# Last block of a fused retention and PReLU kernel: a second group of d_ff tiles by seven products, the second-layer products in another order, the third sums on GpSimd

## The chip, the core and the metric

The kernel runs on one core of one Trainium2 chip. The core has five engines with a queue each, taken in order: TensorE (PE in the profile, with its weight loads as PEld), VectorE (DVE), ScalarE (ACT), GpSimd (POOL) and SyncE (SP, which here only issues transfers). The metric is device time in microseconds (us) of one execution; the times given are medians of several.

## The reference

Eight heads of 64 run a decaying recurrence over 768 steps for four batches; the 3072 rows of 512 that come out go through a two-layer network with a leaky rectifier of its own slope for each of the 2048 hidden columns.

```python
for t in range(S):
    state = gamma * state + einsum('bhd,bhe->bhde', k[:, :, t], v[:, :, t])
    y[:, :, t] = scale * einsum('bhd,bhde->bhe', q[:, :, t], state)
x = y.transpose(0, 2, 1, 3).reshape(B * S, H * D)     # 3072 x 512
h = x @ w_in                                          # d_ff = 2048
g = maximum(h, 0) + alpha * minimum(h, 0)
out = g @ w_out                                       # 3072 x 512, float32
```

## The kernel before

The 3072 rows are worked through in `NBLK` = 6 blocks of 512 rows (n = 0 to 5). A block passes through a first layer (its 512 rows of x, kept transposed as `xT`, times `w_in`, giving `gt`, the hidden values after the rectifier, as 16 tiles f of 128 hidden columns) and a second layer (`gt` times `w_out`). The recurrence of block n+1 is computed in chunks inside the second layer of block n, so that in block 5 nothing but the two layers is left. The order of work on every engine is the order of the calls in the program; a generator is advanced with `tick(gen, m)` by m matmuls.

**First layer of blocks 3 to 5** (`ffn1_mix`). A "full" tile takes four matmuls of 128x512 (`L923`), a negated relu on ScalarE into `hm` (`L906`) and a multiply-add on VectorE (`L910`) that writes `gt`. One group of four tiles (0, 1, 8 and 9) is instead formed by seven products of half-size operands (a Strassen-Winograd scheme) of four 128x256 matmuls each (`L953`, numbers 1 to 7 in `part`). It reads sums of pieces of `w_in` (`wins`, from `win_sum`, formed once on GpSimd in block 2) and sums of pieces of x (`xsum`, from `x_sum`, formed for each block: two on VectorE, two on GpSimd). The products pile up in three PSUM banks; after numbers 1, 6 and 7 ScalarE copies a bank out (`kept`, `L966`), and the next product into that bank waits for that copy. After 2, 7 and 3 VectorE adds another bank to a copy (`L970`); the rectifier of such a sum is a relu on ScalarE some steps later and a pair of operations on GpSimd (`L983`, `L989`), in `ends`. `MIX` says which step is a product of the group and which (0) a full tile.

**Second layer of blocks 1 to 5** (`seven`). Again seven products, each of 16 matmuls of 128x256 (`L790`), first for 128 rows (t = 0) over the eight tiles f, then for the other 128. The operands are quarters of `gt` (`A(i, j)`: rows half i, tiles half j) and of `w_out`, and sums of these: `gs` 0 and 1 (`sm[0]`, `sm[1]`), `third`, and an in-place difference in `gt`, formed by `g_sums(n, part, which, engine)`, where `part` is a half of the tiles (f 0 to 3, or 4 to 7) and `which` is 0 to 3 in that order. In block 5, `gs` 0 and 1 of part 0 are begun inside the first layer (GpSimd, then VectorE), the rest is on VectorE. The order of the products in block 5 is: A(0,0); A(0,1); `sm[1]`; `sm[0]`; `third`; A(1,1); A(0,1) after its in-place difference. Results leave PSUM by ScalarE copies (`kept`, `L808`) and VectorE sums (`os`, `put`, `L820`), and then by stores (`L824`).

`minus` (`L738`) is the one line that records all sums of both kinds; they are told apart by the names of their tiles.

```python
MIX = [1, 2, 0, 5, 6, 0, 7, 0, 0, 4, 3] + 8 * [0]
fts = [f for i in range(2, HF) for f in (i, i + HF)]     # full tiles: 2, 10, 3, 11, ... 7, 15
```

Of the kernel before, what the change touches and what calls it, by code (L numbers as in the profile page):

```python
# [19 lines left out]
def kernel(  # L20
# [761 lines left out]

    def seven(n):
        gt, sm = gts[n], gsum[n]

        def product(bank, a, w, first=False):
            for t in range(2):
                for f in range(HF):
                    bk = bank[t] if isinstance(bank, list) else bank
                    nc.tensor.matmul(  # L790
                        out=bk[:, 256 * t : 256 * t + 256],
                        lhsT=a[:, f, 128 * t : 128 * t + 128],
                        rhs=w[:, f, :],
                        start=first and f == 0 and (t == 0 or bk is not bank),
                        stop=(f == HF - 1),
                        skip_group_check=True,
                    )
                    yield
# [12 lines left out]
        end = n + 1 == NBLK  # L811
# [40 lines left out]
        if end:  # L852
            gen = product(c, A(0, 1), W(1, 1))
            for _ in range(HF):
                yield next(gen)
            store()
            put(0, 1, c, u2, ts=(0,), store=nc.sync)()
            yield from gen
            put(0, 1, c, u2, ts=(1,))()
        else:  # L860
            yield from product(c, A(0, 1), W(1, 1))
            store()
            late_stores.append(put(0, 1, c, u2))

    wins, xsum = [], []

    def win_sum(i, eng):  # L870
        if not wins:
            wins.append(sbp.tile([128, 4, 2, 256], F16, tag="gs2", bufs=1, name="wins"))
        t = wins[0]
        a = [[w_in_all[:, 2 * l : 2 * l + 2, 1024 * j : 1024 * j + 256] for l in range(2)] for j in range(2)]
# [19 lines left out]
        minus(eng, t[:, i], x, y)  # L894


    MIX = [1, 2, 0, 5, 6, 0, 7, 0, 0, 4, 3] + 8 * [0]

    def ffn1_mix(n):
        fts = [f for i in range(2, HF) for f in (i, i + HF)]  # L900
        x = xT[n]
        h, bk, later = {}, {}, []

# [27 lines left out]
            prelu(ft, slice(0, TB), relu(hps, "hm"), hps)  # L931


        def part(s, i):
# [4 lines left out]
            b, w, t = bk[at], wins[0], xsum[0]  # L939
            for ff in range(2):  # L940
                f = slice(128 * ff, 128 * ff + 128)
                f8 = slice(1024 + 128 * ff, 1152 + 128 * ff)
                for kk in range(2):
                    lhsT, rhs = (
                        (w_in_all[:, kk, f], x[:, 0, kk, :]),
                        (w_in_all[:, 2 + kk, f], x[:, 0, 2 + kk, :]),
                        (w[:, 3, kk, f], x[:, 1, 2 + kk, :]),
                        (w_in_all[:, 2 + kk, f8], t[:, 3, kk, :]),
                        (w[:, 0, kk, f], t[:, 0, kk, :]),
                        (w[:, 1, kk, f], t[:, 1, kk, :]),  # L950
                        (w[:, 2, kk, f], t[:, 2, kk, :]),
                    )[i - 1]
                    nc.tensor.matmul(  # L953
                        out=b[:, 256 * ff : 256 * ff + 256],
                        lhsT=lhsT,
                        rhs=rhs,
                        start=first and ff == 0 and kk == 0,
                        stop=kk == 1,
                        skip_group_check=True,
                    )  # L960
                    yield
            if i in (1, 6, 7):
                h[i] = sbp.tile(
                    [128, 512], FP, tag="um1" if i == 6 else "um0", bufs=2, name="kept"
                )
                nc.scalar.activation(out=h[i], in_=b, func=COPY, bias=0.0, scale=1.0)  # L966
            if i in (2, 7, 3):

                to = h[{2: 1, 7: 7, 3: 6}[i]]
                nc.vector.tensor_tensor(out=to, in0=bk["a" if i == 2 else "c"], in1=to, op=ADD)  # L970
                later.append((s, to, {2: (0, 0), 7: (HF, 256), 3: (0, 256)}[i]))
            if i == 4:
                hm = relu(b, "hm")
                for ff in range(2):
                    at = slice(256 * ff, 256 * ff + 256)
                    prelu(HF + ff, slice(0, 256), hm[:, at], b[:, at])

        def ends():
            while later:
                _, to, (f, t) = later.pop(0)  # L980
                hm = relu(to, "uv")
                hv, v = [a.rearrange("p (f t) -> p f t", f=2) for a in (hm, to)]
                nc.gpsimd.tensor_tensor(  # L983
                    out=hv,
# [5 lines left out]
                    out=gt_at(n, slice(f, f + 2), slice(t, t + 256)), in0=hv, in1=v, op=ADD  # L990
                )

        for s, step in enumerate(MIX):
            yield from part(s, step) if step else full()
# [256 lines left out]
    for n in range(1, NBLK):  # L1251
        more = n + 1 < NBLK
        u0 = UB * (n + 1)
        if n == 2:
# [12 lines left out]
                tick(gen, (14, 14, 6, 16)[i])  # L1267
            g_sums(n, 0, 2, G)
            for i in range(4):
                win_sum(i, G)  # L1270
            for _ in gen:
                pass
        elif n > 2:
            gen = ffn1_mix(n)
            tick(gen, 8)
            flush(late_stores)
            if more:
# [20 lines left out]
        if not more:  # L1298
            tick(gen, 4 * HF + 2)
# [2 lines left out]
        if more:  # L1302
# [118 lines left out]
```

## Time and profile before

| | before |
|---|---|
| time, median of 3 runs | 199.31 us (198.13 to 200.34) |
| span of the profiled execution | 196.5 us |
| PE busy | 188.7 us (96%) |
| VectorE busy | 151.4 us (77%) |
| GpSimd busy | 149.0 us (76%) |
| ScalarE busy | 119.1 us (61%) |

The times are taken without the profiler and hold more than the span, which runs from the first to the last instruction of one execution; that execution has no other time of its own than its span. The median is 2.8 us above it. A busy PE is not a PE at its peak. In rows of the timeline the columns are: start, length, engine, line, operation, output and inputs with their shape, count, and in brackets the idle time before it with what ended it.

### The profile page before, as it was taken

What the parts mean: (1) busy time and instruction counts of PE and PEld (TensorE: products, weight loads), DVE (VectorE), ACT (ScalarE), POOL (GpSimd) and SP (SyncE); (2) the same over time, 40 slices, a digit from 0 to 9 for tenths busy, and PEclk for the clock granted to TensorE, in tenths of its full rate; (3) what the DMA queues carried; (4) which work ended last, traced back from release to release, by engine and by line L of the source; (5) the groups of instructions that cost most, each with busy time, mean ns of one, the idle gap of its engine ahead of it and who ended that gap; (6) DMA issues with size and microseconds to landing.
All of it is one profiled execution on the core that took longest, in us unless ns stands there. A gap on an engine that the chain in (4) does not pass through costs nothing.

```text
span 196.5 us, 6453 instructions
## 1 busy us (share of the span) xinstructions
PE 188.7 (96%) x2668; PEld 131.3 (67%) x2668; DVE 151.4 (77%) x258; ACT 119.1 (61%) x265; POOL 149.0 (76%) x151
## 2 busy tenths in 40 slices
PE   7879999999999989999999999999999999999993
PEld 5657544558668878644788754888654888655882
DVE  2697987164989897588978879967789977798922
ACT  3377763238676954477549987749987334686210
POOL 3368989999999576999379999499999296678000
PEclk9999999999999999999999999999999999999999
DMA  6999999999898999999998999992860013100014
GB/s 170 326 361 400 408 384 284 328 360 195 180 244 132 184 306 225 212 282 240 226 222 201 213 224 224 244 215 83 184 189 2 3 57 110 57 0 0 0 58 160
DMA packets 92749, 38.78 MB, mean 197 GB/s; under 512 B 70176, under 2 KB 88624, under 8 KB 92720
## 3 DMA queue, kind: packets, MB, share of 16 engines
q1 hardware_dynamic: 91440, 37.36, 75.8%
q10 hardware_dynamic: 1280, 1.01, 1.6%
q8 instruction: 21, 0.34, 0.7%
q14 instruction: 8, 0.07, 0.1%
HBM read 27.35 MB, written 6.29 MB: 171 GB/s over the span
## 4 chain that ended last, share of the span: by engine, by line
PE 75%; DVE 5%; POOL 5%; DMA 4%; ACT 3%; issue 2%; SPq 2%; POOLq 1%; DVEq 0%; ACTq 0%
PE ops L790 25%; PE hps L620 12%; PE hps L923 11%; PE hps L648 9%; PE ops L715 5%; PE hps L953 3%; DMA qu<-in_q_dram 2%; SPq L340 2%; POOL gt L989 2%; ACT kq L129 2%; PE ops L684 2%; DMA kt<-kq 2%; POOL hm L983 2%; PE ya L522 1%; POOLq L1416 1%
## 5 line engine op out<-in xcount | busy, mean ns | idle before, releaser
L790 PEld LDWEIGHTS <-gt 128*128 128x128 f16 x320 | 30.6, 98 | 4.1
L923 PE MATMUL hps<-xT,win 128*128 128x512 f16 x144 | 33.0, 379 | 0.0
L910 DVE SCALAR_TENSOR_TENSOR gt<-hm,small,hps 128x512 f16<-128x512 f32 (+1 forms) x42 | 28.7, 706 | 5.1 <-ACT hm L906 3.8
L790 PE MATMUL ops<-wout,gt 128*128 128x256 f16 x240 | 28.4, 273 | 0.0
L906 ACT ACTIVATE hm<-hps 128x512 f32<-128x512 f32 x39 | 23.1, 593 | 6.1 <-PE hps L923 5.4
L620 PE MATMUL hps<-xT,win 128*128 128x512 f16 x112 | 24.5, 379 | 0.0
L630 DVE SCALAR_TENSOR_TENSOR gt<-hm,small,hps 128x512 f16<-128x512 f32 x28 | 20.9, 747 | 3.8 <-ACT hm L629 0.9
L923 PEld LDWEIGHTS <-win 128*128 128x128 f16 x144 | 14.1, 98 | 14.4
L137 POOL TENSOR_TENSOR kq<-kqs,tab 128x512 f16<-128x512 f32 x23 | 23.6, 1050 | 0.0
L629 ACT ACTIVATE hm<-hps 128x512 f32<-128x512 f32 x28 | 16.7, 597 | 9.3 <-PE hps L620 9.3
L662 DVE SCALAR_TENSOR_TENSOR gt<-hm,small,hps 128x256 f16<-128x256 f32 x40 | 17.1, 477 | 4.3 <-ACT hm L657 4.3
L808 ACT ACTIVATE kept<-ops 128x512 f32<-128x512 f32 x15 | 9.0, 597 | 18.4 <-PE ops L790 18.4
L620 PEld LDWEIGHTS <-win 128*128 128x128 f16 x112 | 11.0, 98 | 12.8
L217 POOL TENSOR_TENSOR t<-ss,tab 128x256 f16<-128x256 f32 x13 | 8.7, 670 | 14.0 <-DVE ss L215 14.0
L790 PE MATMUL ops<-wsum,gs 128*128 128x256 f16 x160 | 19.1, 273 | 0.2 <-DVE os L820 0.2
L738 POOL TENSOR_TENSOR gt<-gt,gs 128x1024 f16<-128x1024 f16 x8 | 17.0, 2125 | 2.3 <-PE ops L790 2.3
L648 PE MATMUL hps<-xT,win 128*128 128x256 f16 x160 | 18.3, 273 | 0.0
L129 ACT ACTIVATE kq<-kqs,tab 128x64 f16<-128x64 f32 x72 | 18.1, 337 | 0.0
L648 PEld LDWEIGHTS <-win 128*128 128x128 f16 x160 | 15.4, 98 | 2.4
L790 PEld LDWEIGHTS <-gs 128*128 128x128 f16 x160 | 15.1, 98 | 2.4 <-issue 0.4
L820 DVE TENSOR_TENSOR os<-ops,kept 128x512 f32<-128x512 f32 (+1 forms) x17 | 10.5, 624 | 6.5 <-ACT kept L808 4.6
L657 ACT ACTIVATE hm<-hps 128x512 f32<-128x512 f32 x20 | 11.8, 597 | 5.5 <-PE hps L648 3.9
(132 smaller groups left out, 388.5 us busy)
## 6 DMA issues: line engine op xcount, KB each, us to landing
out_dram<-os SPq DMA_DIRECT2D x20, 256.0 KB, 3.5
wi<-in_moe_w_in_dram SPq DMA_DIRECT2D x8, 512.0 KB, 7.7
wo<-in_moe_w_out_dram SPq DMA_DIRECT2D x8, 512.0 KB, 8.5
kqs<-in_k_dram SPq DMA_DIRECT2D x16, 256.0 KB, 4.3
kqs<-in_q_dram SPq DMA_DIRECT2D x16, 256.0 KB, 4.2
vs<-in_v_dram SPq DMA_DIRECT2D x16, 256.0 KB, 4.9
ku<-in_k_dram SPq DMA_DIRECT2D x4, 256.0 KB, 4.1
qu<-in_q_dram SPq DMA_DIRECT2D x4, 256.0 KB, 4.7
```

The source lines that it names most:

```text
L129: eng.activation(out=kqs[u][:, a, h % 4, h // 4, :], in_=staged[u][nm][:, h, :], func=COPY, bias=0.0, scale=tab[:, H * a + h : H * a + h + 1],
L137: eng.tensor_tensor(out=kqs[u][:, a].rearrange("p i r d -> p r i d"), in0=staged[u][nm].rearrange("p (r i) d -> p r i d", i=4), in1=tab[:, ...
L620: nc.tensor.matmul(out=hps, lhsT=w_in_all[:, hp, 128 * ft : 128 * ft + 128], rhs=xT[n][:, :, hp, :], start=(hp == 0), stop=(hp == 3),)
L629: nc.scalar.activation(out=hm, in_=hps, func=RELU, bias=0.0, scale=-1.0)
L630: nc.vector.scalar_tensor_tensor(out=gt_at(n, ft, slice(0, TB)), in0=hm, scalar=oma_sb[:, ft : ft + 1], in1=hps, op0=MULT, op1=ADD,)
L648: nc.tensor.matmul(out=hps[:, 256 * (ft - f0) : 256 * (ft - f0) + 256], lhsT=w_in_all[:, hp, 128 * ft : 128 * ft + 128], rhs=xT[n][:, half ...
L662: nc.vector.scalar_tensor_tensor(out=gt_at(n, f, to), in0=hm[:, at], scalar=oma_sb[:, f : f + 1], in1=hps[:, at], op0=MULT, op1=ADD,)
L738: eng.tensor_tensor(out=out, in0=a, in1=b, op=op)
L790: nc.tensor.matmul(out=bk[:, 256 * t : 256 * t + 256], lhsT=a[:, f, 128 * t : 128 * t + 128], rhs=w[:, f, :], start=first and f == 0 and ( ...
L906: nc.scalar.activation(out=t, in_=src, func=RELU, bias=0.0, scale=-1.0)
L910: nc.vector.scalar_tensor_tensor(out=gt_at(n, f, cols), in0=hm, scalar=oma_sb[:, f : f + 1], in1=src, op0=MULT, op1=ADD,)
L923: nc.tensor.matmul(out=hps, lhsT=w_in_all[:, hp, 128 * ft : 128 * ft + 128], rhs=x[:, :, hp, :], start=(hp == 0), stop=(hp == 3),)
```

## The change

All of it concerns block 5, with sums prepared in block 4.

- A second group of four tiles (2, 3, 10, 11) of block 5's first layer goes by seven products as well. Eight full tiles are left there instead of twelve. `MIX` becomes `TWO`, two lists run one after the other; relus of the sums come two steps after the sum in all cases, and the last sum of the second group is finished on VectorE.
- Its four sums of pieces of `w_in` (`wins1`) are formed on GpSimd in block 4: three after the first half of `third`, the fourth after the last in-place difference.
- In block 5's second layer the eight tiles of each product are taken in the order 4 to 7, 0 to 3. The product of A(1,1) comes third. All four `gs` sums come after the first layer on VectorE, both halves of `third` on GpSimd. The last product goes to banks of its own, and a sum `half` (line 854 of the changed kernel) is formed for it.

```diff
+        end = n + 1 == NBLK
         def product(bank, a, w, first=False):
+            fs = [f ^ 4 if end else f for f in range(HF)]
             for t in range(2):
-                for f in range(HF):
+                for f in fs:
...
         store = put(0, 0, a, s1)
+        if end:
+            d = bank(k + 2, "ops")
+            yield from product(d, A(1, 1), wsum[3], True)
+            d = kept(d, "um1")
         yield from product(b, sm[1], wsum[1])
         u2 = kept(b, "um0")
         store()
         c = bank(k + 1, "ops")
-        if end:
-            c = [c, ps("ops")]
         yield from product(c, sm[0], wsum[0], True)
         yield from product(b, third[0], wsum[2])
+        if end:
+            other = put(1, 0, b, d, SUB)
         u3 = kept(b, "um1")
         store = put(1, 1, c, u3)
+        if end:
+            other()
+            store()
+            half = sbp.tile([128, 512], FP, tag="um0", bufs=2, name="kept")
+            nc.vector.tensor_tensor(out=half, in0=c, in1=u2, op=ADD)
+            e = [bank(k + 3, "ops"), ps("ops")]
+            gen = product(e, A(0, 1), W(1, 1), True)
+            for _ in range(HF):
+                yield next(gen)
+            put(0, 1, e, half, ts=(0,), store=nc.sync)()
+            yield from gen
+            put(0, 1, e, half, ts=(1,))()
+            return
...
-    MIX = [1, 2, 0, 5, 6, 0, 7, 0, 0, 4, 3] + 8 * [0]
+    ONE = [1, 2, 0, 5, 6, 0, 7, 0, 0, 4, 3] + 8 * [0]
+    TWO = [1, 2, 0, 5, 6, 0, 7, 0, 4, 3], [1, 0, 2, 5, 6, 0, 7, 0, 4, 3, 0, 0]
...
-                later.append((s, to, {2: (0, 0), 7: (HF, 256), 3: (0, 256)}[i]))
+                lo = 2 * g
+                later.append((s, to, {2: (lo, 0), 7: (HF + lo, 256), 3: (lo, 256)}[i], g and i == 3))
...
-                _, to, (f, t) = later.pop(0)
+                _, to, (f, t), own = later.pop(0)
                 hm = relu(to, "uv")
+                if own:
+                    for ff in range(2):
+                        at = slice(256 * ff, 256 * ff + 256)
+                        prelu(f + ff, slice(t, t + 256), hm[:, at], to[:, at])
+                    continue
...
-            if later and s - later[0][0] >= (2 if later[0][0] > 1 else 3):
+            if later and s - later[0][0] >= (2 if two or later[0][0] > 1 else 3):
                 ends()
-            if s == 15:
-                g_sums(n, 0, 2 if n + 1 < NBLK else 0, nc.gpsimd)
-            if s == 17 and n + 1 == NBLK:
-                g_sums(n, 0, 1, nc.vector)
+            if s == 15 and not two:
+                g_sums(n, 0, 2, nc.gpsimd)
...
+        if n == NBLK - 2:
+            for i in range(3):
+                win_sum(1, i, G)
         for p, w in (
-            ((0, 1), (1, 0), (1, 1)) if n == 1 else ((None, 0), (None, 1)) if more else ((1, 0), (1, 1))
+            ((0, 1), (1, 0), (1, 1))
+            if n == 1
+            else ((None, 0), (None, 1))
+            if more
+            else ((1, 0), (1, 1), (0, 0), (0, 1))
         ):
             g_sums(n, p, w, V)
         if not more:
-            g_sums(n, 0, 2, V)
-            g_sums(n, 1, 2, V)
+            g_sums(n, 0, 2, G)
+            g_sums(n, 1, 2, G)
...
                 chain(pb, pq, [], [(1, 3, G)], nxt[0:1])
+                if n == NBLK - 2:
+                    win_sum(1, 3, G)
```

GpSimd's queue in block 4, before, from the first half of `third` (gt_3242 is block 4's hidden values, t_21 a state of the recurrence):

```order
L738 TENSOR_TENSOR third<-gt_3242 128x1024
L217 TENSOR_TENSOR t_21_3456<-ss_3454,tab 128x256
L738 TENSOR_TENSOR third<-gt_3242 128x1024
L217 TENSOR_TENSOR t_22_3507<-ss_3505,tab 128x256
L738 TENSOR_TENSOR gt_3242<-gt_3242,gs_3352 128x4x256
```

The same place in the changed kernel:

```order
L738 TENSOR_TENSOR third<-gt_3242 128x1024
L738 TENSOR_TENSOR wins_3446<-win 128x512
L738 TENSOR_TENSOR wins_3446<-wins_3446,win 128x512
L738 TENSOR_TENSOR wins_3446<-win 128x512
L217 TENSOR_TENSOR t_21_3460<-ss_3458,tab 128x256
L738 TENSOR_TENSOR third<-gt_3242 128x1024
```

Three sums of 128x512 now stand between the first half of `third` and the state.

VectorE's queue at the end of block 5's first layer and in its second, before (gt_3856 is the hidden values, gs_3965 and gs_3966 the sums 0 and 1):

```order
L910 SCALAR_TENSOR_TENSOR gt_3856<-hm,small,hps 128x512 x7
L738 TENSOR_TENSOR gs_3966<-gs_3965,gt_3856 128x1024
L910 SCALAR_TENSOR_TENSOR gt_3856<-hm,small,hps 128x512
L738 TENSOR_TENSOR gs_3965<-gt_3856 128x1024
L738 TENSOR_TENSOR gs_3966<-gs_3965,gt_3856 128x1024
L738 TENSOR_TENSOR third<-gt_3856 128x1024 x2
L820 TENSOR_TENSOR os<-ops,kept 128x512
L738 TENSOR_TENSOR gt_3856<-gt_3856,gs_3966 128x4x256 x2
L820 TENSOR_TENSOR os<-ops,kept 128x256 x2
L820 TENSOR_TENSOR os<-kept,ops 128x512
L820 TENSOR_TENSOR os<-ops,kept 128x256 x2
```

The same place in the changed kernel (gt_3861, gs_4018 and gs_4019 are the same three):

```order
L928 SCALAR_TENSOR_TENSOR gt_3861<-hm,small,hps 128x512 x2
L928 SCALAR_TENSOR_TENSOR gt_3861<-hm,small,kept 128x256 x2
L738 TENSOR_TENSOR gs_4018<-gt_3861 128x1024
L738 TENSOR_TENSOR gs_4019<-gs_4018,gt_3861 128x1024
L738 TENSOR_TENSOR gs_4018<-gt_3861 128x1024
L738 TENSOR_TENSOR gs_4019<-gs_4018,gt_3861 128x1024
L819 TENSOR_TENSOR os<-ops,kept 128x512
L738 TENSOR_TENSOR gt_3861<-gt_3861,gs_4019 128x4x256 x2
L819 TENSOR_TENSOR os<-ops,kept 128x512 x2
L854 TENSOR_TENSOR kept<-ops,kept 128x512
L819 TENSOR_TENSOR os<-ops,kept 128x256 x2
```

The four `gs` sums now stand behind all of the rectifier, part 1 first; the two halves of `third` have left the queue (they are the last two entries of GpSimd's); and three sums of 128x512 stand before the last two of 128x256.

More of the change, by code (lines that the diff above doesn't have):

```diff
@@ L793, in product @@
                         rhs=w[:, f, :],
-                        start=first and f == 0 and (t == 0 or bk is not bank),
-                        stop=(f == HF - 1),
+                        start=first and f == fs[0] and (t == 0 or bk is not bank),
+                        stop=(f == fs[-1]),
                         skip_group_check=True,
@@ L851, in seven, with win_sum @@
         store = put(1, 0, u3, d, SUB)
[L852 to L874, printed above, removed]
+        yield from product(c, A(0, 1), W(1, 1))
+        store()
+        late_stores.append(put(0, 1, c, u2))
+    wins, xsum = {}, []
+    def win_sum(g, i, eng):
+        if g not in wins:
+            wins[g] = sbp.tile(
+                [128, 4, 2, 256], F16, tag=("gs2", "wi1")[g], bufs=1, name=f"wins{g}"
+            )
+        t = wins[g]
+        a = [
+            [
+                w_in_all[:, 2 * l : 2 * l + 2, 1024 * j + 256 * g : 1024 * j + 256 * g + 256]
+                for l in range(2)
+            ]
+            for j in range(2)
+        ]
         x, y, op = (
@@ L894, in x_sum, with ffn1_mix @@
         minus(eng, t[:, i], x, y)
-    MIX = [1, 2, 0, 5, 6, 0, 7, 0, 0, 4, 3] + 8 * [0]
-    def ffn1_mix(n):
-        fts = [f for i in range(2, HF) for f in (i, i + HF)]
+    ONE = [1, 2, 0, 5, 6, 0, 7, 0, 0, 4, 3] + 8 * [0]
+    TWO = [1, 2, 0, 5, 6, 0, 7, 0, 4, 3], [1, 0, 2, 5, 6, 0, 7, 0, 4, 3, 0, 0]
+    def ffn1_mix(n, two=False):
+        mix = [i and (g, i) for g, m in enumerate(TWO if two else [ONE]) for i in m]
+        groups = 2 if two else 1
+        fts = [f for i in range(2 * groups, HF) for f in (i, i + HF)]
         x = xT[n]
@@ L991, in ends @@
                 )
[L993 to L995 removed]
+        for s, step in enumerate(mix):
+            yield from part(s, *step) if step else full()
+            if later and s - later[0][0] >= (2 if two or later[0][0] > 1 else 3):
                 ends()
[L997 to L1000 removed]
+            if s == 15 and not two:
+                g_sums(n, 0, 2, nc.gpsimd)
+        ends()
     late_stores = []
@@ L1273 @@
         elif n > 2:
-            gen = ffn1_mix(n)
+            gen = ffn1_mix(n, not more)
             tick(gen, 8)
```

22 lines of the change are left out of this document (11 added, 11 removed).

## Prediction

> **What bounds the kernel now.** I read the page's head first, then the stretches of block 5 (first layer, second layer), then the chain that ended last, then the timelines.
>
> ```profile
> span 196.5 us, 6453 instructions
> PEclk9999999999999999999999999999999999999999
> 165.40:180.40 15.00, 15.00 (x97) 8.72 (x92) 12.82 (x21) 11.20 (x22) 10.46 (x9) 1.00 0.14 46
> 180.40:193.20 12.80, 12.56 (x113) 10.76 (x111) 8.32 (x14) 2.39 (x4) 0.92 (x1) 1.00 0.13 46
> ```
>
> The columns of the last two are the stretch, its length, busy us (and count) of PE, PEld, DVE, ACT and POOL, the clock, and the transfers. TensorE is busy throughout the last 28 us, at full granted clock. But the chain shows that it runs only just ahead of VectorE:
>
> ```profile
> 181.36 0.69 DVE gs L738
> ...
> 185.36 0.61 DVE os L820
> ...
> 186.02 7.16 PE ops L790 x64
> 193.20 0.42 DVE os L820
> ```
>
> It enters PE only at 186.02, from VectorE's `os`. So matmuls saved are worth their time only if the sums come no later. The matmuls of block 5:
>
> ```profile
> 166.92 1.04 PE L953 MATMUL hps<-xT,win 128*128 128x256 f16 x8
> 167.79 1.03 PE L923 MATMUL hps<-xT,win 128*128 128x512 f16 x4
> 173.49 7.07 PE L923 MATMUL hps<-xT,win 128*128 128x512 f16 x32
> 180.39 3.67 PE L790 MATMUL ops<-wout,gt 128*128 128x256 f16 x32
> 183.91 1.91 PE L790 MATMUL ops<-wsum,gs 128*128 128x256 f16 x16
> 186.02 1.91 PE L790 MATMUL ops<-wsum,gs 128*128 128x256 f16 x16 [0.20 <-DVE os L820]
> ```
>
> From start to start a 128x256 takes (167.79-166.92)/8 = 0.109 us, a 128x512 (180.39-173.49)/32 = 0.216; a product of the second layer 16 x 0.109 = 1.74. The lengths printed also hold the last matmul's way to PSUM.
>
> **1. Matmuls: -0.40.** Four full tiles, 16 x 0.216 = 3.45, become seven products, 28 x 0.109 = 3.05. The second layer keeps its seven products.
>
> **2. Window sums in block 4: +1.4.** The engines there now:
>
> ```profile
> 150.93 2.12 POOL L738 TENSOR_TENSOR third<-gt 128x1024 f16<-128x1024 f16 x1
> 156.92 0.61 POOL L217 TENSOR_TENSOR t<-ss,tab 128x256 f16<-128x256 f32 x1 [3.88 <-DVE ss L215]
> 153.50 1.23 DVE L738 TENSOR_TENSOR gs<-gt 128x2048 f16<-128x2048 f16 x1
> 154.76 1.22 DVE L738 TENSOR_TENSOR gs<-gs,gt 128x2048 f16<-128x2048 f16 x1
> 156.06 1.80 PE L790 MATMUL ops<-wsum,gs 128*128 128x256 f16 x15
> L738 POOL TENSOR_TENSOR wins<-win x2: 1157/1158/1158, 90.4 to 92.8; 128x512 f16<-128x512 f16 x2
> ```
>
> GpSimd is idle for 3.88 us, and three sums of 1.16 would fit. But they lie over VectorE's two `gs` sums, and an f16 sum on VectorE does not run beside GpSimd here:
>
> ```profile
> 166.44 0.43 DVE L738 TENSOR_TENSOR xsum<-xT 128x512 f16<-128x512 f16 x1
> 166.97 1.28 DVE L738 TENSOR_TENSOR xsum<-xT,xsum 128x512 f16<-128x512 f16 x1
> 166.82 1.15 POOL L738 TENSOR_TENSOR xsum<-xT 128x512 f16<-128x512 f16 x1 [1.89 <-ACT xT L600]
> 137.79 1.13 DVE L738 TENSOR_TENSOR xsum<-xT 128x512 f16<-128x512 f16 x1
> 138.59 0.79 POOL L217 TENSOR_TENSOR t<-ss,tab 128x256 f16<-128x256 f32 x1
> ```
>
> The same sum takes 0.43 alone, and 1.28 when GpSimd is in an operation: it ends at 168.25, 0.28 after GpSimd's end at 167.97. The other case ends 0.33 after 138.59, where GpSimd's next operation begins, and that one takes 0.79 instead of 0.61. So the two engines take turns, the waiting one next, and one that has waited finishes about 0.14 sooner after its release than its length alone. The Trainium skill ("SBUF — State Buffer", the section on two separate sides) calls this an exclusive lock on a shared port pair, held for a whole instruction, with the loser fully blocked. By it the whole length would follow each release, and 0.14 more would be paid for each of the seven waits counted in this forecast, at most 1.0 more, 207.1; both rows end sooner than that, and I take theirs.
>
> In turns: first window sum 153.05 to 154.21; first `gs` until 154.21 + 1.23 - 0.14 = 155.30; second window sum (it reads the first, so GpSimd can't go on at once) until 156.32; second `gs` until 157.40 instead of 154.76 + 1.22 = 155.98. The `sm[1]` product starts at 156.06, right behind it, and is full time for PE afterwards: +1.4. Bounds: 0, if they ran side by side, and 3 x 1.16 = 3.5. GpSimd's own queue behind it (a state, `third`, two differences) shifts by as much as PE does. The fourth sum, 1.16, goes into the 1.89 us of idle time before the `xsum` at 166.82: nothing.
>
> **3. Waits inside the first layer: +1.56.** ScalarE gets 22 instructions for 19, and their order changes.
>
> ```profile
> 168.77 0.68 DVE L970 TENSOR_TENSOR kept<-hps,kept 128x512 f32<-128x512 f32 x1
> 169.79 0.60 ACT L966 ACTIVATE kept<-hps 128x512 f32<-128x512 f32 x1 [0.34 <-PE hps L953]
> 170.28 0.62 ACT L906 ACTIVATE hm<-kept 128x512 f32<-128x512 f32 x1
> 170.44 0.61 PE L953 MATMUL hps<-xsum,wins 128*128 128x256 f16 x4
> 170.98 1.04 POOL L983 TENSOR_TENSOR hm<-hm,small 128x512 f32<-128x512 f32 x1 [1.49 <-ACT hm L906]
> 172.10 1.27 POOL L989 TENSOR_TENSOR gt<-hm,kept 128x512 f16<-128x512 f32 x1
> ```
>
> Group 1: the relu of the first sum (ready at 168.77 + 0.68 = 169.45) now stands ahead of copy 6, which moves from 169.79 to about 170.06; product 7 waits for it, and it runs as soon as it can already (170.44): +0.28. Product 3 follows product 7 after one full tile instead of two; copy 7 ends at 171.98, VectorE's sum at 172.71; product 3 is due at 170.72 + 0.44 + 0.86 + 0.44 = 172.46, so about +0.30. Group 2 repeats both more tightly. Laid out with the same lengths, copy 6 starts at 176.03; behind it stand the relu of a sum that VectorE ends at 176.72, a tile's relu at 177.29, and copy 7 from 177.79 to 178.39, while product 4 is due at 177.97: +0.47. Product 3, behind VectorE's sum of that copy, loses as much again, 0.5. Below, 0: ScalarE may get through as it does now; above, twice the sum, as each wait is an ending of a chain of three engines. I take the sum. With the -0.40 the second layer starts 1.16 later.
>
> **4. Tile order in the first product: +0.43.** The tile computed last but one (7) was read by the eighth matmul, now by the fourth, 4 x 0.109 earlier.
>
> ```profile
> 175.84 5.27 DVE L910 SCALAR_TENSOR_TENSOR gt<-hm,small,hps 128x512 f16<-128x512 f32 x7
> 180.59 0.60 ACT L906 ACTIVATE hm<-hps 128x512 f32<-128x512 f32 x1 [0.27 <-PE hps L923]
> L738 POOL TENSOR_TENSOR third<-gt x6: 2119/2125/2135, 88.4 to 157.5; 128x1024 f16<-128x1024 f16 x6
> ```
>
> It is written at 175.84 + 5.27 = 181.11, and the eighth matmul runs at 180.39 + 0.76 = 181.15: no slack today.
>
> **5. `gs` sums against `third`: +2.9, less 0.37.** Count from the start of the second layer, T (180.39 today, 181.5 then). The last tile's relu starts at T + 0.2, the relu of the last sum at about T + 0.75, its two VectorE operations end at T + 2.5. Both the `gs` sums and GpSimd's `third` wait for these (GpSimd's pairs of 2.35, as from 170.98 to 173.37, are through by T + 1.8: the second starts at 173.9, four end at 183.3), so they set out together. In turns: sum 1 T + 3.2; `third` a T + 5.15 (2.12 - 0.14); sum 2 T + 5.7; `third` b T + 7.7; sum 3 T + 8.2; sum 4, unopposed, T + 8.95. The `sm[1]` product, now fourth, starts at T + 0.43 + 3 x 1.74 = T + 5.65 and reads sum 4 with its fifth matmul, T + 6.1: a wait of 2.9. Side by side sum 4 would be ready at T + 5.2: wait 0. So 0 to 2.9; the `xsum` rows say 2.9. The wait at 186.02 goes (186.02 - 183.91 - 1.74 = 0.37), as `os` is then long written. `third` is ready well ahead of its product.
>
> **6. The end: +1.28.** After the `third` product two products follow today; then only one, with more behind it.
>
> ```profile
> 165.57 0.42 DVE L599 TENSOR_TENSOR xT<-ya,zs 128x256 f16<-128x256 f32 x1 [0.30 <-PE yb L293]
> 166.02 0.38 ACT L600 ACTIVATE xT<-ya 128x256 f16<-128x256 f32 x1 [0.32 <-DVE xT L599]
> 191.46 0.69 DVE L820 TENSOR_TENSOR os<-kept,ops 128x512 f32<-128x512 f32 x1 [0.36 <-PE ops L790]
> 193.20 0.42 DVE L820 TENSOR_TENSOR os<-ops,kept 128x256 f32<-128x256 f32 x1 [0.45 <-PE ops L790]
> ```
>
> Two readers of one bank are put in sequence, as with `ya` here (ScalarE starts when VectorE has ended), so from the `third` product's end, with 0.03 to 0.04 from one engine to the next as in these two rows: `os` 0.72, copy 0.64, `os` and `half` 0.65 + 0.68 (the second starts 0.08 before the first ends), two small sums 0.38 + 0.42, together 3.5. The last product alone would end it at 1.74 + 0.46 = 2.2. Bounds 0.6 (copy beside the `os`) and 1.3. The last store is the same one; 193.62 to the span's end stays.
>
> **Sum:** -0.40 + 1.4 + 1.56 + 0.43 + 2.9 - 0.37 + 1.28 = +6.8: span 196.5 to 203.3. The median of the runs is 2.8 above the span; 199.31 + 6.8 = 206.1.
>
> **The rivals.** (a) Only one of the two collisions costs its price, since engines arrive a few tenths apart: 206.1 - 2.9 = 203.2, or - 1.4 = 204.7. Against: both sides of each are queued behind the same event or in the open. (b) The matmuls decide, and it is not slower: VectorE and GpSimd don't get in each other's way and ScalarE keeps up, so PE runs from 166.92 without a gap. Then -0.40 - 0.37, with the end's +1.28, gives +0.5, 199.8. It decides at T + 6.1: sum 4 before that or not. For it: PE 12.56 busy of 12.80 today. Against: 166.97, and no slack at 156.06, 170.44 and 181.15. (c) The clock falls in the gap of 2.9 us:
>
> ```profile
> PE wps L1026 <- DVE small L1020: 1.3, 1, 1.3
> ```
>
> The longest wait of PE is 1.3 us so far, at full clock throughout, so the rows can't exclude it. At half clock 12 + 32 matmuls more at 0.109 and the last product's later end, 0.45, give +5.2: 211.3. The Trainium skill ("TensorE: Matmul & The Clock Gate", Part 1) has the clock halved after an idle window of about 3.4 us; the gap is shorter, so by that rule the clock stays.
>
> **How the numbers follow.** Within 1% (2 us, about what this kernel's measurement can tell) lies 197.3 to 201.3. Forecast 0.71, on its own 204.5 to 207.8; (a) 0.14; (b) 0.09; (c) 0.04; 0.02 for a gain over 1%, which no step here gives. So slower 0.89, same 0.09, faster 0.02. The range takes in (a) and both sides of the forecast: 202.5 to 207.8.
>
> **What would show it.** In block 4: `gs` of 1.8 and 2.6 us instead of 1.23, and PE idle before the `sm[1]` product. In block 5: `gs` sums of 2.5 us on VectorE between two `third` of 2.6 on GpSimd; a PE wait of nearly 3 us on DVE `gs`; waits before products 7, 4 and 3 of the first layer; PE finished 1.5 us before VectorE. I am wrong if `gs` keeps its 0.69 beside `third`.

## The result, and the profile after

| | before | after |
|---|---|---|
| time, median of 6 runs each | 199.46 us (198.13 to 200.79) | 207.62 us (206.63 to 210.32) |
| span of the profiled execution | 196.5 us | 205.8 us |
| PE / VectorE / GpSimd / ScalarE busy in it | 188.7 / 151.4 / 149.0 / 119.1 us | 189.9 / 157.5 / 162.6 / 121.3 us |

The changed kernel takes 1.0433 times as long [1.0373, 1.0492]: slower, as forecast, and by more. On the 199.31 us from which the prediction counted, that is 207.9 us (206.7 to 209.1 by the interval), where 206.1 and a range of 202.5 to 207.8 were given. The comparisons leave out the slowest, disturbed runs; where such a run was the profiled one, only its trace is read, stretch by stretch.

Four rows of PE's waits in the profile of after, with total, times and longest in us (rows between them that before has as well, 1.3 us and less, are left out):

```profile
PE ops L792 <- DVE gs L738: 3.7, 2, 2.5
PE hps L648 <- issue: 1.8, 1, 1.8
PE hps L972 <- ACT kept L985: 0.4, 1, 0.4
PE ops L792 <- DVE gt L928: 0.3, 1, 0.3
```

Three of the four were forecast: two on `gs` (block 4 and block 5), one inside the first layer, one for the tile that the first product reads early. The second row was not; it stands at 47.8 us, long before anything that was changed. Where they lie on PE's timeline of after (start, length, instruction, and in brackets the idle time before it):

```profile
49.64 3.65 PE L648 MATMUL hps<-xT,win 128*128 128x256 f16 x32 [1.83 <-issue]
...
155.06 3.67 PE L792 MATMUL ops<-wout,gt 128*128 128x256 f16 x32
159.91 3.23 PE L792 MATMUL ops<-wsum,gs 128*128 128x256 f16 x28 [1.19 <-DVE gs L738]
...
170.78 1.04 PE L972 MATMUL hps<-xT,win 128*128 128x256 f16 x8
...
182.34 0.60 PE L972 MATMUL hps<-xsum,win 128*128 128x256 f16 x4 [0.37 <-ACT kept L985]
183.23 0.60 PE L972 MATMUL hps<-xT,wins 128*128 128x256 f16 x4 [0.30 <-DVE kept L989]
...
185.40 0.49 PE L792 MATMUL ops<-wout,gt 128*128 128x256 f16 x3
186.23 3.34 PE L792 MATMUL ops<-wout,gt 128*128 128x256 f16 x29 [0.34 <-DVE gt L928]
189.40 1.91 PE L792 MATMUL ops<-wsum,gt 128*128 128x256 f16 x16
191.15 0.60 PE L792 MATMUL ops<-wsum,gs 128*128 128x256 f16 x4
194.27 3.23 PE L792 MATMUL ops<-wsum,gs 128*128 128x256 f16 x28 [2.52 <-DVE gs L738]
197.34 1.91 PE L792 MATMUL ops<-wsum,third 128*128 128x256 f16 x16
```

Two rows of PE's timeline of before complete those of the prediction, the start of block 4's second layer and of the last product but one:

```profile
152.55 3.67 PE L790 MATMUL ops<-wout,gt 128*128 128x256 f16 x32
...
189.51 1.91 PE L790 MATMUL ops<-wsum,gt 128*128 128x256 f16 x16
```

All that the change touches lies behind the start of block 4's second layer (152.55 and 155.06). From there to the end of VectorE's last sum before took 193.62 - 152.55 = 41.07 us, and after, whose last sum ends at 203.18, took 48.12. By landmarks, with the prediction's terms:

| stretch | before | after | difference | forecast |
|---|---|---|---|---|
| block 4, first two products, until `sm[1]` (term 2) | 3.51 | 4.85 | +1.34 | +1.4 |
| from there to block 5 | 10.86 | 10.87 | +0.01 | 0 |
| block 5, first layer (terms 1 and 3) | 13.47 | 14.62 | +1.15 | +1.16 |
| second layer, first two products (term 4) | 3.52 | 4.00 | +0.48 | +0.43 |
| third to fifth product (term 5) | 5.60 | 7.94 | +2.34 | +2.53 |
| sixth product until the last sum (term 6) | 4.11 | 5.84 | +1.73 | +1.28 |
| together | 41.07 | 48.12 | +7.05 | +6.8 |

Behind the last sum 2.62 us follow instead of 2.88, so the changed part costs +6.8, the forecast sum. That it agrees to 0.1 is in part luck: term 6 came out 0.45 over its forecast, while term 5 and the part behind the last sum came out 0.19 and 0.26 under theirs. The spans differ by 9.3, because this execution came to the landmark 2.5 us late. And the medians differ by 8.2, not 6.8. Both surpluses were open at this point. (The execution of after that was profiled took 207.49 us, 1.7 more than its span. If before's differ by the same, some 1.1 of the 2.8 us between its span and its median come from a profiled execution that started early.)

VectorE and GpSimd in the two collisions, in after (the sums in between left out):

```profile
156.00 1.76 DVE L738 TENSOR_TENSOR gs<-gt 128x2048 f16<-128x2048 f16 x1
157.80 2.06 DVE L738 TENSOR_TENSOR gs<-gs,gt 128x2048 f16<-128x2048 f16 x1
...
187.76 0.68 DVE L738 TENSOR_TENSOR gs<-gt 128x1024 f16<-128x1024 f16 x1
188.47 2.49 DVE L738 TENSOR_TENSOR gs<-gs,gt 128x1024 f16<-128x1024 f16 x1
190.88 2.60 DVE L738 TENSOR_TENSOR gs<-gt 128x1024 f16<-128x1024 f16 x1
193.52 0.69 DVE L738 TENSOR_TENSOR gs<-gs,gt 128x1024 f16<-128x1024 f16 x1
...
199.69 0.69 DVE L819 TENSOR_TENSOR os<-ops,kept 128x512 f32<-128x512 f32 x1 [3.68 <-issue]
201.04 0.69 DVE L819 TENSOR_TENSOR os<-ops,kept 128x512 f32<-128x512 f32 x1 [0.66 <-ACT kept L810]
```

GpSimd's timeline of after, in the same two places:

```profile
155.52 1.15 POOL L738 TENSOR_TENSOR wins<-win 128x512 f16<-128x512 f16 x1
156.76 2.01 POOL L738 TENSOR_TENSOR wins<-wins,win 128x512 f16<-128x512 f16 x1
158.74 2.13 POOL L738 TENSOR_TENSOR wins<-win 128x512 f16<-128x512 f16 x1
...
187.91 5.03 POOL L738 TENSOR_TENSOR third<-gt 128x1024 f16<-128x1024 f16 x2 [0.76 <-DVE gt L928]
```

This is the taking of turns that the prediction laid out. `gs` ends at 188.44, 190.96, 193.48 and 194.21, where T = 185.40 gave 188.6, 191.1, 193.6 and 194.35: each 0.1 to 0.2 early. The middle two print 2.5 us for 0.69 us of work, since they stand in the engine while GpSimd holds its turn.

### The profile page after: what moved, and what is told of

It is laid out like the page before. It is cut to its first block, busy times and chain, and to the rows that moved or that the text cites. A ratio compares the mean times of both kernels' runs of the same rounds, so it can differ in the third digit from the quotient of the medians.

```text
span 205.8 us, 6492 instructions
## 1 busy us (share of the span) xinstructions
PE 189.9 (92%) x2680; PEld 132.0 (64%) x2680; DVE 157.5 (77%) x260; ACT 121.3 (59%) x269; POOL 162.6 (79%) x160
## 5 line engine op out<-in xcount | busy, mean ns | idle before, releaser
L928 DVE SCALAR_TENSOR_TENSOR gt<-hm,small,hps 128x512 f16<-128x512 f32 (+1 forms) x40 | 26.7, 691 | 6.4 <-ACT hm L924 5.3
L941 PE MATMUL hps<-xT,win 128*128 128x512 f16 x128 | 30.1, 379 | 0.0
L620 PE MATMUL hps<-xT,win 128*128 128x512 f16 x112 | 24.9, 380 | 0.3 <-POOL win L1078 0.3
L924 ACT ACTIVATE hm<-hps 128x512 f32<-128x512 f32 x36 | 21.3, 594 | 5.8 <-PE hps L941 5.1
L810 ACT ACTIVATE kept<-ops 128x512 f32<-128x512 f32 x16 | 9.6, 597 | 24.8 <-PE ops L792 20.8
L629 ACT ACTIVATE hm<-hps 128x512 f32<-128x512 f32 x28 | 16.7, 597 | 10.0 <-PE hps L620 9.0
L941 PEld LDWEIGHTS <-win 128*128 128x128 f16 x128 | 12.5, 98 | 11.9
L620 PEld LDWEIGHTS <-win 128*128 128x128 f16 x112 | 10.9, 98 | 13.6 <-POOL win L1078 1.1
L738 POOL TENSOR_TENSOR third<-gt 128x1024 f16<-128x1024 f16 x8 | 17.8, 2225 | 0.9 <-DVE gt L928 0.8
L648 PEld LDWEIGHTS <-win 128*128 128x128 f16 x160 | 15.5, 98 | 4.2 <-issue 1.8
L819 DVE TENSOR_TENSOR os<-ops,kept 128x512 f32<-128x512 f32 (+1 forms) x17 | 11.1, 655 | 7.0 <-issue 3.7
```

The lines of the kernel that those rows point to most:

```text
L620: nc.tensor.matmul(out=hps, lhsT=w_in_all[:, hp, 128 * ft : 128 * ft + 128], rhs=xT[n][:, :, hp, :], start=(hp == 0), stop=(hp == 3),)
L629: nc.scalar.activation(out=hm, in_=hps, func=RELU, bias=0.0, scale=-1.0)
L648: nc.tensor.matmul(out=hps[:, 256 * (ft - f0) : 256 * (ft - f0) + 256], lhsT=w_in_all[:, hp, 128 * ft : 128 * ft + 128], rhs=xT[n][:, half ...
L738: eng.tensor_tensor(out=out, in0=a, in1=b, op=op)
L924: nc.scalar.activation(out=t, in_=src, func=RELU, bias=0.0, scale=-1.0)
L928: nc.vector.scalar_tensor_tensor(out=gt_at(n, f, cols), in0=hm, scalar=oma_sb[:, f : f + 1], in1=src, op0=MULT, op1=ADD,)
```

## The experiments

Ratios are to runs of before on the same chip. "Landmark" is the start of block 4's second layer.

**The late start: both kernels again, unchanged.**

> The kernel before, unchanged, to see how far the part up to the start of block 4's second layer (152.55 us in the first profile of before, 155.06 in that of the changed kernel, though the program is the same up to there) wanders by itself. Theory A (the 2.5 us between the two profiles are not from the change but from transfers and code loading that differ from execution to execution): this profile starts block 4's second layer anywhere from 152.5 to 155, ratio 1.00. Theory B (the longer program of the change loads its code differently): this profile starts it at 152.5 +- 0.4 again, without a pause of PE near 47 us.

> The changed kernel, unchanged. Theory A: block 4's second layer starts anywhere from 152.5 to 155, and the pause of 1.8 us near 48 us need not come back; from that start to the last VectorE sum 48.1 us again (41.1 before). Theory B: the pause comes back, start at 155 +- 0.4.

Before again: 199.32 us, ratio 1.0029 [0.9981, 1.0077], landmark at 154.00 instead of 152.55, and 41.07 us from there to the last sum, as in the first profile. After again: 206.75 us, ratio 1.0431 [1.0315, 1.0547], landmark at 153.73, 48.15 us. The 1.83 us pause at 47.8 us did not come back at that length. Over the 13 profiles of this study the landmark lies between 152.2 and 156.2, with (but for one kernel) the same instructions ahead of it. So the start wanders by itself, in both kernels, and one profile's span is no measure of a change of a few us; the stretch behind the landmark repeats within 0.03 us in the two profiles of each.

**Term 5: the `third` sums on VectorE.**

```diff
-            g_sums(n, 0, 2, G)
-            g_sums(n, 1, 2, G)
+            g_sums(n, 0, 2, V)
+            g_sums(n, 1, 2, V)
```

> The changed kernel with both halves of the third sum of block 5 back on VectorE, behind the gs sums. Theory (VectorE and GpSimd take turns on the f16 sums): the wait of 2.5 us of PE within the sm[1] product is gone, each gs sum takes 0.69, and the time falls by 2.5 to 2.9 us against the changed kernel (ratio to before about 1.030). Rival (the gs sums come too late by themselves, being all behind the rectifier): a wait of 2 us or more stays and the time falls by less than 0.5.

203.07 us, ratio 1.0216 [1.0111, 1.0320]. VectorE's timeline in this kernel:

```profile
188.96 0.68 DVE L738 TENSOR_TENSOR gs<-gt 128x1024 f16<-128x1024 f16 x1
189.67 0.69 DVE L738 TENSOR_TENSOR gs<-gs,gt 128x1024 f16<-128x1024 f16 x1
190.28 0.68 DVE L738 TENSOR_TENSOR gs<-gt 128x1024 f16<-128x1024 f16 x1
191.00 0.69 DVE L738 TENSOR_TENSOR gs<-gs,gt 128x1024 f16<-128x1024 f16 x1
191.61 1.29 DVE L738 TENSOR_TENSOR third<-gt 128x1024 f16<-128x1024 f16 x2
```

And PE's:

```profile
192.35 3.66 PE L792 MATMUL ops<-wsum,gs 128*128 128x256 f16 x32
```

All six sums go through in 3.9 us, where GpSimd took 5.03 for two, and `sm[1]` and `sm[0]` run in one piece. Landmark to last sum: 201.34 - 156.23 = 45.11, 3.0 less. The collision is shown as the cause of the gap. The ratio fell by 0.0215, 4.3 us: more than the trace, but each of the two ratios is uncertain by 0.01 (2 us), so this is only a hint that the gap costs more than its length.

**Term 2: without the second group's window sums.** The sums of `w_in` for group 2 are left out; its products read group 1's.

```diff
-            b, w, t = bk[at], wins[g], xsum[0]
+            b, w, t = bk[at], wins[0], xsum[0]
...
-        if n == NBLK - 2:
-            for i in range(3):
-                win_sum(1, i, G)
...
-                if n == NBLK - 2:
-                    win_sum(1, 3, G)
```

> The changed kernel without the four window sums of group 2 in block 4; group 2's products read group 1's sums, so the sums of the second group's weights are left out of the computation. Theory (the gs sums of block 4 wait for them in turns): gs takes 1.23 and 1.22 again, PE has no wait before block 4's sm[1] product, and the time falls by 1.3 us (ratio to before about 1.037). Rival (the second layer of block 4 has slack for it later): gs is short again, but the first layer of block 5 starts no earlier against the start of block 4's second layer, 15.7 us, as in the changed kernel.

205.62 us, ratio 1.0348 [1.0257, 1.0438]. In block 4 `sm[1]` follows without a wait (159.06 - 155.56 = 3.50, as in before), so the term is shown. But landmark to last sum came out at 48.46, more than after's 48.12. PE's timeline of this kernel:

```profile
190.30 0.60 PE L792 MATMUL ops<-wsum,gs 128*128 128x256 f16 x4
193.42 4.90 PE L792 MATMUL ops<-wsum,gs 128*128 128x256 f16 x28 [2.52 <-DVE gs L738]
```

The windows of this kernel from 193.42 on (stretch, its length, busy us of PE, PEld, DVE, ACT and POOL, the granted clock, the share of the DMA engines, what they moved in GB/s):

```profile
193.42:194.71 1.29, 1.29 (x12) 1.17 (x13) 1.29 (x3) 0.00 (x0) 0.00 (x0) 1.00 0.00 0
194.71:198.12 3.41, 3.41 (x18) 2.37 (x17) 0.45 (x1) 0.60 (x1) 0.00 (x0) 0.50 0.24 82
198.12:200.00 1.88, 1.88 (x19) 1.67 (x17) 0.00 (x0) 0.00 (x0) 0.00 (x0) 1.00 0.00 0
```

The same 28 matmuls that took 3.23 us in after take 4.90 here: behind the same gap of 2.52 us the granted clock is 0.50 for 3.41 us. Less these 1.67 the stretch is 46.79, 1.33 under after's. The fall of the clock that rival (c) named happens, then, at least in some executions, though not until the end of the kernel.

**The clock: filling the gap.** Twelve matmuls of zeros into a bank of their own, between the third product, A(1,1), and `sm[1]`, keep PE busy while it would wait; nothing else moves.

```diff
+            z = ps("wps")
+            for _ in range(12):
+                nc.tensor.matmul(out=z, lhsT=wz[:, 0:128], rhs=wz, start=True, stop=True)
         yield from product(b, sm[1], wsum[1])
```

> The changed kernel with twelve matmuls of zeros (128x512, 2.6 us, into a bank nobody reads) between the A(1,1) and the sm[1] product of block 5, where TensorE otherwise waits 2.5 us. No engine gets its operands earlier. Theory (in some executions the clock is halved after that wait, which adds about 1.7 us to those, and with transfers at the start makes the 1.3 us by which the median moved beyond the sum): the sm[1] product goes on at the same time after the start of block 4's second layer as before to 0.2 us, the clock is 1.00 as long as matmuls run in every execution, and the median falls by 0.5 to 1.2 us against the changed kernel (206.75 to 207.62). Rival (the clock plays no part; all of the 1.3 us arises before block 4): median as the changed kernel's, within 0.3.

206.49 us, ratio 1.0362 [1.0326, 1.0399], on another chip than after's repetition. On PE's timeline `sm[1]` and `sm[0]` run at full clock:

```profile
190.29 2.75 PE L842 MATMUL wps<-wz 128*128 128x512 f16 x12
192.88 3.76 PE L792 MATMUL ops<-wsum,gs 128*128 128x256 f16 x32
```

Landmark to last sum is 48.15, as in after: the filling took nothing away but the halved clock. The ratio leaned towards the clock, with intervals that overlap after's. So both were run side by side on one chip:

> The changed kernel again, on the same chip as the next, with the wait of 2.5 us of TensorE open. Theory (the clock is halved after the wait in some executions and costs those about 1.7 us): the executions fall in two kinds, ratio to before 1.040 to 1.046, and the mean granted clock is at or under 0.995 in half of them. Rival (no part of the clock): ratio within 0.002 of the next kernel's.

> As the last, with the wait filled by matmuls of zeros. Theory: ratio to before 1.034 to 1.038 (the sum of the trace, 6.8 us, is 1.034), lower than the kernel with the open gap by 0.004 or more. Rival: the same ratio within 0.002.

The gap left open: 207.14 us, ratio 1.0416 [1.0372, 1.0461]. Filled: 205.71 us, ratio 1.0338 [1.0294, 1.0381]. The difference of 0.0078 is 1.6 us, more than the 0.004 that the theory gave, though the intervals overlap slightly. And 1.0338 is what the trace's +6.8 makes of 199.4 us: 1.034. The profile with the open gap shows the halved clock (landmark to last sum 49.79 = 48.12 + 1.67), the one with the filled gap doesn't (48.16). But the executions with the open gap do not fall in two kinds by time, as the theory had it. The mean granted clock of each execution is known, and one stretch of 3.41 us at half clock makes 0.992 of 205 us. The three executions at or under that (0.985, 0.986, 0.992) took 206.32, 207.02 and 208.87 us, the other three 206.76, 207.26 and 207.41. So these six don't show the price of 1.67 us, and a start that wanders by 4 us can hide it. The windows of the kernel with the open gap:

```profile
189.36:192.77 3.41, 0.90 (x9) 0.59 (x7) 3.38 (x4) 0.45 (x1) 1.44 (x1) 1.00 0.00 0
192.77:196.18 3.41, 3.41 (x18) 2.44 (x17) 1.10 (x2) 0.60 (x1) 0.00 (x0) 0.50 0.24 81
199.60:203.01 3.41, 0.92 (x9) 0.58 (x6) 2.35 (x5) 0.60 (x1) 0.00 (x0) 1.00 0.44 156
203.01:205.30 2.29, 0.00 (x0) 0.00 (x0) 0.00 (x0) 0.00 (x0) 0.00 (x0) 0.50 0.33 115
```

The clock falls 0.64 us after PE is at work again, stays at half for 3.41 us, and falls once more 10.24 = 3 x 3.41 us after the first fall, each time behind a 3.41 us stretch in which PE was busy for 0.9 us.

**Term 6: `half` ahead of the chain.** The sum `half` is formed before the `third` product ends, and that product is copied out by ScalarE first.

```diff
-        yield from product(b, third[0], wsum[2])
         if end:
-            other = put(1, 0, b, d, SUB)
+            half = sbp.tile([128, 512], FP, tag="um0", bufs=2, name="kept")
+            nc.vector.tensor_tensor(out=half, in0=c, in1=u2, op=ADD)
+        yield from product(b, third[0], wsum[2])
...
-            other()
+            other = put(1, 0, u3, d, SUB)
             store()
-            half = sbp.tile([128, 512], FP, tag="um0", bufs=2, name="kept")
-            nc.vector.tensor_tensor(out=half, in0=c, in1=u2, op=ADD)
+            other()
```

> The changed kernel, with half formed ahead of the third product, and the copy of the third product's bank made first, from which both os sums of 128x512 are formed. Theory (the end is a chain of VectorE and ScalarE behind the third product): from the third product's last matmul to the end of the last VectorE sum 2.7 us instead of 3.5, the start of block 4's second layer to there 47.3 instead of 48.13. Rival (PE's last product sets the end): 48.1 again.

A single run: 206.07 us. From the end of the `third` product to the end of the last sum 201.27 - 198.59 = 2.68, against 203.18 - 199.25 = 3.93 in after: -1.25. About 0.9 of that is the chain. The other 0.35 is the pause marked "issue" in front of after's `os` (199.69, which is 0.44 behind the product's end): here it falls on `half`, off the path, and the copy begins 0.09 behind the product. The clock halved in this run too (28 matmuls in 4.90); landmark to last sum is 48.54, or 46.87 less 1.67.

**Terms 1 and 3: one group of seven only, the rest as changed.**

```diff
-            if s == 15 and not two:
+            if s == 15 and n + 1 < NBLK:
                 g_sums(n, 0, 2, nc.gpsimd)
...
-            gen = ffn1_mix(n, not more)
+            gen = ffn1_mix(n)
```

> The changed kernel, with block 5's first layer as in the kernel before (one group, twelve full tiles), everything else as changed, window sums in block 4 included (nobody reads them). Theory (the second group costs 1.15 us of ScalarE and VectorE waits net of its 0.40 saved, and by its last sum on VectorE sets third and the gs sums out together): the first layer of block 5 takes 13.47 us again instead of 14.62, third is mostly done before the gs sums start, the wait within sm[1] falls from 2.5 to under 0.3, and the start of block 4's second layer to the last VectorE sum takes 43.8 us. Rival (all four gs sums behind the rectifier are enough to make the wait): 1.15 less only, 47.0.

A single run: 203.64 us. Block 5's first layer takes 184.01 - 170.53 = 13.48, before's 13.47. The gap is gone as well, though `third` is still on GpSimd. GpSimd's timeline in this kernel:

```profile
182.81 4.21 POOL L738 TENSOR_TENSOR third<-gt 128x1024 f16<-128x1024 f16 x2
```

And VectorE's:

```profile
185.62 1.95 DVE L738 TENSOR_TENSOR gs<-gt 128x1024 f16<-128x1024 f16 x1
187.60 0.69 DVE L738 TENSOR_TENSOR gs<-gs,gt 128x1024 f16<-128x1024 f16 x1
```

Without the second group `third` begins 1.2 us ahead of the second layer (184.01) instead of 2.5 us behind it (185.40), and one `gs` pays 1.3 us instead of two paying 1.8 and 1.9. Landmark to last sum is 44.32, against 48.12: the second group, which saves 0.40 us of matmuls, costs 3.8 us net by what it makes the other engines do, and when. The window sums in block 4 are still formed here.

**All of it mended at once.** Window sums formed early on VectorE, another order of steps in both groups, tiles in the old order, the `gs` sums in pairs of parts, `third` on VectorE, `sm[0]` behind `third` (the lines of the last, and those that take the window sums out of block 4, are left out here).

```diff
-            fs = [f ^ 4 if end else f for f in range(HF)]
+            fs = list(range(HF))
...
-    TWO = [1, 2, 0, 5, 6, 0, 7, 0, 4, 3], [1, 0, 2, 5, 6, 0, 7, 0, 4, 3, 0, 0]
+    TWO = [1, 2, 5, 6, 0, 7, 0, 4, 0, 3], [1, 2, 5, 6, 0, 0, 7, 0, 4, 0, 3, 0]
...
+    for i in range(4):
+        win_sum(1, i, V)
...
-            else ((1, 0), (1, 1), (0, 0), (0, 1))
+            else ((0, 0), (1, 0), (0, 1), (1, 1))
...
-            g_sums(n, 0, 2, G)
-            g_sums(n, 1, 2, G)
+            g_sums(n, 0, 2, V)
+            g_sums(n, 1, 2, V)
```

> The changed kernel with four mends: the window sums of group 2 on VectorE near 34 us, where it waits; full tiles spread between the products so that each copy has time; third on VectorE; the third product ahead of the sm[0] one, so that only os, half and two small sums follow the latter. Theory (the mechanisms named are all there is): from the start of block 4's second layer to the last VectorE sum 42.0 us against 41.07 before and 48.13 changed, so that even mended the second group pays nothing; ratio to before 1.003 to 1.01. Rival (the 0.40 us of matmuls come through once the waits are gone): 40.7 or less.

200.06 us, ratio 1.0045 [1.0008, 1.0083]; landmark to last sum 41.93, 0.86 more than before. PE's timeline:

```profile
187.90 1.91 PE L792 MATMUL ops<-wsum,gs 128*128 128x256 f16 x16
190.58 1.91 PE L792 MATMUL ops<-wsum,third 128*128 128x256 f16 x16 [0.77 <-ACT kept L810]
```

Nearly all of the 6.8 us is undone, but nothing is won. What is left contains one new wait: `third` goes into the bank of the product just ahead of it and waits for ScalarE's copy.

**Before with the new end.** The order of products and the `half` of the changed kernel, `sm[0]` behind `third`, put into the kernel before, with one group.

```diff
+            d = bank(k + 2, "ops")
+            yield from product(d, A(1, 1), wsum[3], True)
+            d = kept(d, "um1")
         yield from product(b, sm[1], wsum[1])
...
+            yield from product(b, third[0], wsum[2])
+            u3 = kept(b, "um1")
+            put(1, 0, u3, d, SUB)()
+            yield from product(c, sm[0], wsum[0], True)
...
```

> The kernel before with only the order of the second layer in block 5 changed: A(1,1) third, third sum's product ahead of the sm[0] one, half formed for the last product in banks of its own; sums, tiles and first layer as before. Theory (the product moved ahead gives VectorE 1.7 us more for the sums, which takes away the 0.37 us wait, and with os, half and two small sums behind the sixth product the end costs nothing): start of block 4's second layer to the last VectorE sum 40.7 us instead of 41.07, time within 0.3% of before. Rival (the new order itself costs at the end): 41.5 or more.

200.09 us, ratio 1.0044 [1.0000, 1.0087], 41.62 us from landmark to last sum: a miss. The wait of 0.37 at 186.02 in before is gone, and the same wait on the copy as in the last kernel (0.75 before the `third` product) has come in its place. None of the kernels run here beats before.

## Why the prediction was right and where it was wrong

- **Bound and sign.** PE only just ahead of the other engines, with no slack for more sums: right. Undoing the second group alone gives back 3.8 of 7.05 us, `third` on VectorE alone 3.0; both take away the gap, so the two don't add up.
- **Terms 1 and 3 (+1.16):** +1.15 measured, with the two named waits of PE in group 2 at 0.37 and 0.30; one group brings 13.48 back.
- **Term 2 (+1.4):** +1.34 measured, gone without the window sums. The first `gs` prints 1.76 for 1.8. The second prints 2.06 where 2.6 was given as a sign: that figure is counted from 154.76, while by the prediction's own layout the sum starts at 155.30, which makes 2.1.
- **Term 4 (+0.43):** +0.48, with 0.34 of it idle time on `gt`. No run undoes it alone.
- **Term 5 (+2.53):** +2.34; the wait is 2.52 idle, or 2.7 between starts, for 2.9. The lock that the Trainium skill describes ("SBUF — State Buffer", the section on two separate sides) is what the rows show. The whole length of the waiting sum behind each release is not: `gs` ends 0.54 behind GpSimd's (193.48 - 192.94), where 0.68 is its length alone.
- **Term 6 (+1.28):** mis-sized, +1.73 measured. The chain of sums took 3.93 for the forecast 3.5; 0.35 of that is VectorE's pause before `os`, which no row of before had let expect.
- **Rivals (a) and (b)** did not occur: both collisions cost their price, and sum 4 was ready at T + 8.8, not before T + 6.1.
- **What failed is the step that left the clock out of the sum**: rival (c) got 0.04 at a price of 5.2, and the clock was held to stay because "the gap is shorter" than 3.4 us. Of the five profiles with the open gap three show the halved clock behind it (without window sums, with the early `half`, and the last of after), and after's first two don't. It costs 1.67, not 5.2, as the clock is back after 3.41 us. With the gap filled the ratio is 1.0338 and 1.0362, against 1.034 for the forecast sum; left open it is 1.0416 to 1.0433. So 206.1 was about the time with the clock at full, and the median lay about 1.4 us above the sum. The forecast and (c) were kept apart as cases, while they belong to one: a gap of that length brings the clock with it in part of the executions.
- **What stays open:** whether the clock is all of that 1.4. Of the 16 executions of the changed kernel 7 have a mean granted clock of 0.992 or less, and a stretch at half clock may also lie elsewhere; so at most 0.44 of them paid 1.67, 0.7 us on average. Of the 12 with the gap filled 1 is as low. No run shows where the other half of the surplus comes from; with a start that wanders by 4 us, it may be the spread of few executions.

The page of the Trainium skill cited for that rule ("TensorE: Matmul & The Clock Gate", Part 1) also states that the window of 3413 ns is free-running and isn't reset when a kernel starts. That part of the rule was overlooked. The windows agree with a grid of that length: stretches at half clock of 3.41 us, falls at whole multiples of it. In the kernel with one group the clock is halved once near the start and once at the very end, as its windows show:

```profile
13.36:16.77 3.41, 1.96 (x111) 1.48 (x107) 2.41 (x6) 2.60 (x6) 1.33 (x3) 1.00 1.00 321
16.77:20.18 3.41, 3.32 (x57) 2.33 (x47) 1.57 (x3) 1.83 (x5) 2.52 (x8) 0.50 1.04 385
197.66:201.07 3.41, 0.00 (x0) 0.00 (x0) 0.99 (x3) 0.00 (x0) 0.00 (x0) 1.00 0.46 157
201.07:201.90 0.83, 0.00 (x0) 0.00 (x0) 0.00 (x0) 0.00 (x0) 0.00 (x0) 0.50 0.00 0
```

201.07 - 16.77 = 184.30 = 54 x 3.413. A window need not be idle throughout, either: behind the open gap PE was busy for 0.9 us of the window before the fall. In the windows of after's own profile the grid cuts the same gap in two:

```profile
189.35:192.76 3.41, 2.40 (x22) 1.90 (x20) 3.41 (x2) 0.60 (x1) 3.41 (x2) 1.00 0.00 0
192.76:196.17 3.41, 1.90 (x18) 1.71 (x19) 3.22 (x5) 0.30 (x1) 0.17 (x1) 1.00 0.02 5
199.59:203.00 3.41, 1.40 (x13) 1.00 (x11) 2.56 (x5) 0.60 (x1) 0.00 (x0) 1.00 0.32 113
203.00:205.70 2.70, 0.00 (x0) 0.00 (x0) 0.18 (x1) 0.00 (x0) 0.00 (x0) 0.50 0.44 152
```

With 1.0 and 1.5 us idle in two neighbouring windows the clock stayed; with 2.0 idle, behind PE's end, it fell. If the limit lies between (it can't be one limit for all matmuls, as the last section shows), a gap of 2.52 us halves the clock unless the grid cuts it near its middle: from (2 x 1.5 - 2.52)/3.41 to (2 x 2.0 - 2.52)/3.41, an estimated 0.14 to 0.43 of the executions escape, and the mean price is 1.67 x 0.57 to 0.86 = 0.95 to 1.4 us. That is more than the 0.7 that the clocks of the executions allow, and reaches the measured 1.4 to 1.6 only at its upper end, so the share is not settled. The limit itself was not measured by an experiment of its own.

## What to carry to other kernels

Cost a saved matmul against what its sums make the other engines do, and lay these out in turns where two engines can't run side by side: here 0.40 us of matmuls were bought with 6.8 us. A wait of TensorE has two prices, its length and the clock behind it; below the clock's window the second is a chance, not zero, and belongs into the sum at its share. Compare stretches between landmarks of two traces, not spans: the changed stretch repeated within 0.04 us at full clock, while the start of the same program wandered by 4.

## What the runs showed of the hardware that was not expected

- The clock's fall comes after the gap, not in it: 0.35 us (early `half`), 0.64 and 1.29 us after PE was at work again, in three profiles, and the matmuls that pay are those behind. How much work counts as busy isn't settled: in the kernel with one group the window from 13.36 with 1.96 us of PE, mostly 64x64 matmuls, was followed by half clock, while 1.90 us of 128x256 in after was not.
- VectorE paused for about 0.35 us, marked "issue", before the first instruction behind its last long idle time in after and in the kernels with its gap open or filled (`os`; in the early-`half` kernel `half`). It did not at that place with `third` on VectorE (0.09 behind the product), and with one group a pause of 0.44 came before the last two sums instead. The cause stays open, as does that of the wandering start.
